# Moving ten loads of folded weights behind the normalization's last store, and one subtraction two steps forward, in a fused attention and MLP kernel

## The chip, the cores and the metric

The kernel runs on one core of a Trainium2 chip. The metric is the device time of one execution in microseconds (us); the number given for a kernel is the median of its runs. Five engines work side by side, each through its own queue in order: TensorE (PE in the profile; PEld is its weight load), VectorE (DVE), ScalarE (ACT), GpSimd (POOL) and SyncE (SP), which here issues all DMAs.

## The reference

A token row of x (2048 tokens, 640 features) is normalized twice over, and the sum of the input, a linear attention and an MLP is returned, all in float32:

```python
x = A_x
xn = _layernorm(x, axis=-1)
return x + _A_ref(xn, A_wqkv, A_w_phi, A_wo) + _B_ref(xn, B_w1, B_b1, B_w2, B_b2)
```

`_B_ref` normalizes again, multiplies by w1 (640 x 1728), applies gelu and multiplies by w2 (1728 x 640). `_A_ref` projects to q, k and v (32 heads of 20), and takes features of q and k:

```python
pq = jnp.einsum("bhsd,hdf->bhsf", q, w_phi)
phi_q = jnp.concatenate([_softmax(pq, axis=-1), _softmax(-pq, axis=-1)], axis=-1)
kv = jnp.einsum("bhsf,bhsd->bhfd", phi_k, v)
num = jnp.einsum("bhqf,bhfd->bhqd", phi_q, kv)
```

and divides num by the matching sum of features, before the last projection wo.

## The kernel before

Every float32 operand is split into a high and a low part, and a product is three matmuls (high by high, high by low, low by high; `mm3`, lines 62 to 64). Tokens are held transposed, in four blocks of 512. The program has three stages:

- **The MLP of blocks 0 and 1**, up to about 217 us. The hidden layer is cut in chunks of 128 columns, two to a group; groups 2 to 5 are done by `cycle` with fewer products (sums of weights and of tokens), group 6 by the plain `passes`. In `second`, five products of a group go to the PSUM banks 5, 6 and 7 in turn, and VectorE adds each to `acc` (line 312), which frees the bank: the fourth product waits for the first addition, the fifth for the second.
- **The projections and features of all tokens**, to about 450 us. Their first products read `wkh` and `wkl`, the two tiles of `wkv_`.
- **The MLP of blocks 2 and 3 beside the attention, and the output.**

In the first stage the order of PE, VectorE, ScalarE and GpSimd is as the code is traced; only SyncE's order is set by a scheduler from the dependencies. Side work is written as generators: PE's code calls `next(mlp.beside)` after each three matmuls, and one such step lets the side work trace a few instructions. `prep` is such a side work and runs through groups 2 to 6. It does, in this order:

- **The subtraction** (line 680): `wpt` holds w_phi of all heads (loaded at line 576); VectorE subtracts its first column from the others. Before it `prep` lets four steps go by.
- **The folds** (`folds`): PE multiplies pieces of wk and wq (`raw`, line 581) with `wpt` (line 611), ScalarE and VectorE split the results (lines 629 and 631), and SyncE stores them to DRAM (`wk_dram`, `wq_dram`, line 636).
- **The normalization of blocks 2 and 3**, ten pieces of 128 features by 512 tokens. A piece is loaded (line 673) into one of three `raw` buffers; GpSimd subtracts the mean (line 694), VectorE multiplies by the scale (702), ScalarE makes the high part in `xs` (708), VectorE the low part in place (711), and SyncE stores both to `y_dram` (line 713), the high part (`yh`) first. The load of a piece takes the buffer of the piece three before it, so it waits for that one's low store (`yl`). The pieces are called first to tenth below.

Beside the last of `prep` runs `last_weights`, in group 6. For each of five rows kc it loads the V part of the weights (line 820, `wkl<-wv`), splits it on ScalarE and VectorE (lines 502 and 505), and loads the folded high and low parts of wk from DRAM (line 823, `wkh<-wkh` and `wkl<-wkl`, 256 KB each), ten loads in all. Behind them on SyncE come the folded weights of wq (line 856).

Each DMA signals one of eight semaphores (DMAHW0 to DMAHW7), in turn, and waits until the DMA eight before it, which had the same one, has landed.

Of the kernel before, what the change touches and what calls it, by code (L numbers as in the profile page):

```python
# [25 lines left out]
F1, F2 = 16 * H, 3 * H  # L26
CB = [F1, F1 + 2 * F2 + 15 * DH, F1 + 2 * F2 + D]
# [11 lines left out]
def f(ap):  # L39
    return ap.bitcast(F32)  # L40
# [3 lines left out]
def tile_kernel(ctx: ExitStack, tc: tile.TileContext, x, xT, wkT, wqT, wv, wphi, wo, w1, b1, w2, b2,  # L44
                ident, mmask, emask, vsel, out):
    nc = tc.nc
# [33 lines left out]
    y_dram = [[tc.dram_tile([P, KC, 512], F32, name=f"y{p}{b}") for p in "hl"] for b in range(2)]  # L80
    wq_dram = [tc.dram_tile([P, KC, F1], F32, name=f"wq{p}") for p in "hl"]
    wv_dram = tc.dram_tile([P, KC, D], F32, name="wv_")
    wk_dram = [tc.dram_tile([P, KC, F1], F32, name=f"wk{p}") for p in "hl"]
# [40 lines left out]
    def stats(ts, xp, xbs, turned=False):  # L124

        t0, n = ts[0], len(ts)
        st = xp.tile([P, n, 2, 6], F32, name="st", bufs=1 if n == 8 else 2)
        for i, (t, xb) in enumerate(zip(ts, xbs)):
            for h in range(2):
                nc.vector.bn_stats(st[:, i, h, :], xb[:, h * 320:(h + 1) * 320])  # L130
            nc.vector.bn_aggr(mv[:, t, :], st[:, i, :, :])
            yield


        ts = slice(t0, t0 + n)
        q = xp.tile([P, 2, n], F32, name="q", bufs=2)
        nc.vector.tensor_scalar(q[:, 1, :], mv[:, ts, 1], 0.25 * (1 + EPS), 0.25 * EPS * EPS, op0=ALU.mult, op1=ALU.add)
        nc.vector.tensor_scalar(q[:, 0, :], mv[:, ts, 1], 0.25, 0.25 * EPS, op0=ALU.mult, op1=ALU.add)
        yield

        sr = xp.tile([P, 2, n], F32, name="sr", bufs=3)
        rr = xp.tile([P, 2, n], F32, name="rr", bufs=2)
        nc.scalar.activation(sr, q, AF.Sqrt)
        nc.vector.reciprocal(rr, sr)
        nc.vector.tensor_tensor(rr, rr, q, op=ALU.mult)
        if turned:
            nc.vector.scalar_tensor_tensor(sr, sr, -1.0, rr, op0=ALU.mult, op1=ALU.subtract)
        else:
            nc.vector.tensor_tensor(sr, sr, rr, op=ALU.add)
        nc.vector.reciprocal(ry[:, ts], sr[:, 1, :])  # L150
        yield
        ra = xp.tile([P, n], F32, name="ra", bufs=2)
        nc.vector.reciprocal(ra, sr[:, 0, :])
        nc.vector.tensor_tensor(rs_all[:, ts], sr[:, 1, :], ra, op=ALU.mult)
# [27 lines left out]
    def rows(xp, ptile):  # L182

        sc = xp.tile([P, 2, 2, 4], F32, name="sc", bufs=1)
        nc.vector.tensor_copy(sc[:, :, 0, :], mv[:, 8:16, 0].rearrange("p (b t) -> p b t", b=2))
        nc.vector.tensor_copy(sc[:, :, 1, :], ry[:, 8:16].rearrange("p (b t) -> p b t", b=2))
        for _ in range(4):
            yield
        ps = ptile()
        nc.tensor.transpose(ps[:16, :P], sc.rearrange("p b a t -> p (b a t)"), idt)  # L190
        sr = xp.tile([16, P], F32, name="sr16", bufs=1)
        nc.vector.tensor_copy(sr, ps[:16, :P])
        nc.sync.dma_start(r_dram, sr)

    def row_pair(b, mr):

        nc.sync.dma_start(mr, r_dram[8 * b - 16:8 * b - 8].rearrange("r t -> (r t)").unsqueeze(0).to_broadcast([P, 8 * P]))
        return mr.rearrange("p (a t) -> p a t", a=2)
# [126 lines left out]
    def finish(p):  # L325
        for _ in p:
            pass
# [164 lines left out]
    def at_steps(*events):  # L492

        n = 0
        for when, what in sorted(events, key=lambda e: e[0]):
            while n < when:
                n += 1
                yield
            what()

    def hi(t, src, eng=None):
        return lambda: nc.scalar.activation(t[0], src, AF.Copy)

    def lo(t, src, eng):
        return lambda: eng.tensor_tensor(t[1], src, f(t[0]), op=ALU.subtract)
# [72 lines left out]
    def raws(n, g):  # L578
        raw = fp.tile([P, D], F32, name="raw")
        if g < 5:  # L580
            nc.sync.dma_start(raw, {"k": wkT, "q": wqT}[n][g * G6:g * G6 + P, :])
        else:
            nc.sync.dma_start(raw[:2 * DH], wkT[5 * G6:])
            nc.sync.dma_start(raw[2 * DH:], wqT[D - P + 2 * DH:])
        return raw
# [64 lines left out]
    def ahead(loads, n):  # L650

        todo, ready = iter(loads), []
        for _ in loads:
            while len(ready) <= n:
                load = next(todo, None)
                if load is None:
                    break
                ready.append(load())
            yield ready.pop(0)

    def more_stats():

        def load(t):
            xb = fp.tile([P, D], F32, name="xs", bufs=3)
            nc.sync.dma_start(xb, x[t * P:(t + 1) * P, :])
            return xb

        yield from stats(range(8, 16), fp, ahead([lambda t=t: load(t) for t in range(8, 16)], 2))

    def prep():  # L670
        def load(b, c):
            xc = fp.tile([P, D], F32, name="raw")[:, :512]
            nc.sync.dma_start(xc, xT[c * P:(c + 1) * P, b * 512:(b + 1) * 512])
            return xc

        todo = [(b, c) for b in range(2, 4) for c in range(KC)]
        loads = ahead([*(lambda job=job: raws(*job) for job in jobs), *(lambda job=job: load(*job) for job in todo)], 1)
        for _ in range(4):
            yield
        nc.vector.tensor_tensor(wpt[:, :, :, 1:], wpt[:, :, :, 1:], wpt[:, :, :, 0:1].to_broadcast([P, 6, 6, DF]), op=ALU.subtract)  # L680
        more = chain(more_stats(), rows(fp, mlp.px))
        for i, _ in enumerate(folds(loads)):
            if i % 10 in (5, 7, 9):
                next(more, None)
            yield
        fs.close()
        finish(more)
        mrs = [row_pair(b, fp.tile([P, 2, 512], F32, name="t", bufs=2).rearrange("p a c -> p (a c)")) for b in range(2, 4)]
        for _ in range(6):
            yield  # L690

        def centred(b, c):
            xc = next(loads)
            nc.gpsimd.tensor_tensor(xc, xc, mrs[b - 2][:, 0], op=ALU.subtract)
            return xc

        following = centred(*todo[0])
        for _ in range(4):
            yield
        for i, (b, c) in enumerate(todo):  # L700
            xc = following
            nc.vector.tensor_tensor(xc, xc, mrs[b - 2][:, 1], op=ALU.mult)  # L702
            yield
            if i + 1 < len(todo):
                following = centred(*todo[i + 1])
            yield
            hi = fp.tile([P, D], F32R, name="xs", bufs=3)[:, :512]
            nc.scalar.activation(hi, xc, AF.Copy)
            for _ in range(2):
                yield  # L710
            nc.vector.tensor_tensor(xc.bitcast(F32R), xc, f(hi), op=ALU.subtract)  # L711
            for p, src in enumerate((f(hi), xc)):
                nc.sync.dma_start(y_dram[b - 2][p][:, c, :], src)
            for _ in range(4):
                yield

# [8 lines left out]
    def cycle(g, other, side):  # L725
# [78 lines left out]
        return mlp.second(g, 1, parts, ws)  # L804

    before, side = p11, prep()
    for g in range(2, 6):
        before = cycle(g, before, side)
# [2 lines left out]
    kvw = wkv.enter_context(tc.tile_pool(name="wkv", bufs=1, side="right", reuse_waits="tile"))  # L811
    wkv_ = [kvw.tile([P, KC, CB[2]], F32R, name=f"wk{p}") for p in "hl"]

    def last_weights():

        events = []
        for kc in range(KC):
            k, v = slice(0, F1), slice(F1 + 2 * F2, CB[2])
            raw = f(wkv_[1][:, kc, v])
            events += [(2 * kc, lambda kc=kc, raw=raw: nc.sync.dma_start(raw, wv_dram[:, kc])),  # L820
                       (2 * kc + 7, hi([wkv_[0][:, kc, v]], raw)),
                       (2 * kc + 8.5, lo([wkv_[0][:, kc, v], wkv_[1][:, kc, v]], raw, nc.vector)),
                       *((2 * kc + 10 + p, lambda kc=kc, p=p: nc.sync.dma_start(f(wkv_[p][:, kc, k]), wk_dram[p][:, kc])) for p in range(2))]
        return at_steps(*events)

    mlp.beside = both(last_weights(), side)
    ws = [ready[c][0] for c in (12, 13)]
    for b in range(2):
# [33 lines left out]
    for i in range(2):  # L862
        v = vp.tile([P, 11 * VS], F32R, name=f"v{i}")
# [121 lines left out]
    for t, i in [(t, i) for t in range(13) for i in range(4)] + [(13, 0), (13, 1), (13, 2), (14, 0), (14, 1), (13, 3), (14, 2), (15, 0), (15, 1),  # L985
                                                                  (14, 3), (15, 3), (15, 2)]:
        if (t, i) in ((4, 0), (8, 0)):
            b = t // 4 + 1
# [27 lines left out]
        if i == 0 and t in (1, 2, 3, 6, 7):  # L1016

            kc = (1, 2, 3, 6, 7).index(t)
# [536 lines left out]
```

## Time and profile before

| | us |
|---|---|
| median of 3 runs | 716.82 (716.45 to 717.29) |
| the profiled execution | 716.18 |
| its span, first to last instruction | 714.4 |
| PE busy | 701.8 (98%) |
| VectorE, GpSimd, ScalarE busy | 507.7, 434.5, 353.0 |

In the profile's rows a line is a start (us from the span's start), a duration (us), an engine, a line of the kernel, an operation and its tiles (out<-in); in brackets stands how long the engine had been idle before it, and whose work ended that. SPq is SyncE's queue: an entry is the issue of a DMA and not its transfer. Buffer numbers are left out of names: `raw` is any of its three buffers, and `bank` any PSUM bank. In the chain of waits a DMA's length goes from its issue to its landing.

### The profile page before, as it was taken

Reading aid. Unit: us, or ns where it says so; the run is one execution under the profiler, and the core shown is the slowest. Engines: PE = TensorE matmul, PEld = TensorE weight load, DVE = VectorE, ACT = ScalarE, POOL = GpSimd, SP = SyncE. Lnnn points to the kernel's source line nnn. Section 1 sums busy time; section 2 is a strip of 40 time slices with the busy share of each in tenths; the row PEclk is TensorE's granted clock in tenths of the full one; section 3 lists DMA queues with packets and bytes.
Section 4 is the critical chain, followed back from the end, with each engine's and each line's share of the span. In section 5 each row is a group of like instructions: output and inputs, shape, how many; then the busy total and the mean of one; then the engine's idle time right before and its main releaser. Section 6 shows DMA issues by size and latency. Waiting matters only on the chain.

```text
span 714.4 us, 9919 instructions
## 1 busy us (share of the span) xinstructions
PE 701.8 (98%) x3368; PEld 592.1 (83%) x3368; DVE 507.7 (71%) x842; ACT 353.0 (49%) x624; POOL 434.5 (61%) x405
## 2 busy tenths in 40 slices
PE   8999999999899999999999999999999999999998
PEld 7887888878678888888888888888888888888886
DVE  7876775597474788888978887745565646778653
ACT  7843546445433464454445547556565556551310
POOL 2576424675231897797787879656677777563400
PEclk9999999999999999999999999999999999999999
DMA  9615968456753223624600705674444753163222
GB/s 333 259 40 182 268 186 233 112 179 213 284 200 129 82 79 153 167 93 166 147 2 1 184 1 189 151 220 131 132 120 128 206 150 112 42 232 124 89 74 88
DMA packets 77895, 105.05 MB, mean 147 GB/s; under 512 B 22885, under 2 KB 46069, under 8 KB 76221
## 3 DMA queue, kind: packets, MB, share of 16 engines
q1 hardware_dynamic: 77844, 104.43, 46.3%
q8 instruction: 26, 0.43, 0.2%
q14 instruction: 25, 0.20, 0.1%
HBM read 71.43 MB, written 34.61 MB: 148 GB/s over the span
## 4 chain that ended last, share of the span: by engine, by line
PE 85%; DVE 5%; issue 3%; DMA 3%; ACT 2%; POOL 2%; POOLq 0%; ACTq 0%; SPq 0%; DVEq 0%
PE bank L62 25%; PE bank L63 25%; PE bank L64 25%; PE bank L946 3%; PE bank L611 2%; PE bank L1175 1%; PE bank L1174 1%; DMA raw<-in_xT 1%; DMA wkl<-wv__79 1%; DVE st L130 1%; PE bank L307 1%; PE bank L308 1%; DVE m L754 1%; DVE raw L711 1%; DVE raw L702 1%
## 5 line engine op out<-in xcount | busy, mean ns | idle before, releaser
L62 PE MATMUL bank<-m,w 128*128 128x512 f32 x266 | 105.5, 397 | 5.0 <-DVE acc L312 4.7
L62 PE MATMUL bank<-y,w 128*128 128x512 f32 (+1 forms) x270 | 105.1, 389 | 0.0
L63 PE MATMUL bank<-y,w 128*128 128x512 f32 (+1 forms) x270 | 104.9, 389 | 0.0
L64 PE MATMUL bank<-y,w 128*128 128x512 f32 (+1 forms) x270 | 104.8, 388 | 0.0
L64 PE MATMUL bank<-m,w 128*128 128x512 f32 x266 | 103.7, 390 | 0.0
L63 PE MATMUL bank<-m,w 128*128 128x512 f32 x262 | 102.1, 390 | 0.0
L312 DVE TENSOR_TENSOR acc<-bank,acc 128x512 f32<-128x512 f32 x120 | 80.9, 681 | 18.8 <-PE bank L64 13.8
L62 PE MATMUL bank<-wkh,y 128*128 128x512 f32 (+2 forms) x240 | 87.6, 365 | 0.0
L63 PE MATMUL bank<-wkl,y 128*128 128x512 f32 (+2 forms) x240 | 87.1, 363 | 0.0
L64 PE MATMUL bank<-wkh,y 128*128 128x512 f32 (+2 forms) x240 | 86.9, 362 | 0.0
L911 POOL TENSOR_TENSOR m<-m,mx 128x640 f32<-128x640 f32 (+2 forms) x48 | 44.6, 942 | 42.7 <-DVE mx L899 42.7
L892 ACT ACTIVATE m<-bank 128x512 f32<-128x512 f32 (+1 forms) x64 | 26.4, 439 | 85.7 <-PE bank L64 62.4
L62 PEld LDWEIGHTS bank<-m,w 128*128 128x128 f32 x266 | 50.0, 188 | 17.3 <-DVE acc L312 6.8
L1168 POOL TENSOR_TENSOR e<-e,m 128x512 fp32r<-128x512 f32 (+1 forms) x28 | 40.0, 1431 | 38.4 <-ACT m L1167 32.3
L64 PEld LDWEIGHTS bank<-y,w 128*128 128x128 f32 x270 | 51.1, 189 | 10.4
L63 PEld LDWEIGHTS bank<-y,w 128*128 128x128 f32 x270 | 51.1, 189 | 10.3
L62 PEld LDWEIGHTS bank<-y,w 128*128 128x128 f32 x270 | 51.0, 189 | 10.4
L64 PEld LDWEIGHTS bank<-m,w 128*128 128x128 f32 x266 | 49.9, 188 | 10.5
L918 DVE TENSOR_REDUCE sm<-m 128x64 f32<-128x1280 f32 x32 | 47.3, 1479 | 15.9 <-ACT m L916 15.6
L63 PEld LDWEIGHTS bank<-m,w 128*128 128x128 f32 x262 | 49.3, 188 | 9.5
L916 ACT ACTIVATE m<-m,rs_all 128x1280 f32<-128x1280 f32 x32 | 43.8, 1368 | 22.0 <-POOL m L911 21.9
L56 POOL TENSOR_TENSOR w<-r,w 128x640 fp32r<-128x640 f32 x31 | 48.5, 1583 | 7.8 <-ACT w L53 7.6
(260 smaller groups left out, 1638.2 us busy)
## 6 DMA issues: line engine op xcount, KB each, us to landing
r<-in_w SPq DMA_DIRECT2D x43, 320.0 KB
e<-e SPq DMA_DIRECT2D x40, 256.0 KB
e<-acc SPq DMA_DIRECT2D x52, 160.0 KB
acc<-in_xT SPq DMA_DIRECT2D x4, 1280.0 KB
a<-in_w SPq DMA_DIRECT2D x9, 320.0 KB
xb<-in_x SPq DMA_DIRECT2D x8, 320.0 KB
xs<-in_x SPq DMA_DIRECT2D x8, 320.0 KB
raw<-in_xT SPq DMA_DIRECT2D x10, 256.0 KB
```

The source lines that it names most:

```text
L56: eng.tensor_tensor(lo, src, f(hi), op=ALU.subtract)
L62: nc.tensor.matmul(ps, lh, rh, start=first, stop=False, **kw)
L63: nc.tensor.matmul(ps, lh, rl, start=False, stop=False, **kw)
L64: nc.tensor.matmul(ps, ll, rh, start=False, stop=last, **kw)
L312: nc.vector.tensor_tensor(acc[b][:, m, :], pw, acc[b][:, m, :], op=ALU.add)
L611: nc.tensor.matmul(ps[:, c + i * kd:c + (i + 1) * kd], raw[n, g][:, (kc + i) * P:(kc + i + 1) * P], wpt[:, g, :kd // DF, 1:], start=True, ...
L892: return nc.scalar.activation(p3[:, :, c], ps.rearrange("p (h f) -> p h f", h=H), AF.Copy).ins
L911: subs[n, t] = nc.gpsimd.tensor_tensor(ep[:, s], a, b, op=ALU.subtract)
L916: exps[n, t] = nc.scalar.activation(e, e, AF.Exp, scale=rs_all[:, t:t + 1])
L918: nc.vector.tensor_reduce(sm, e.rearrange("p s (h f) -> p (s h) f", f=DH), axis=AX, op=ALU.add)
L946: nc.tensor.matmul(kvp[g // 2][:P, (g % 2) * 240:(g % 2) * 240 + 240].rearrange("p (s f) -> p s f", s=4), v[:, g * VS:g * VS + P], ft[:, : ...
L1168: nc.gpsimd.tensor_tensor(pl, e, f(ph), op=ALU.subtract)
```

## The change

Two edits. The subtraction on `wpt` is made after two of the four steps that `prep` lets go by, instead of after all four. And the ten loads of folded wk weights are now issued behind the normalization's last store: `prep` notes each store in `stored`, and the loads are traced four steps later than before and with `issue_after`, which puts them behind the store that was noted last on SyncE's queue. No instruction is added or taken away.

```diff
+    stored = [None]
+
     def prep():
...
-        for _ in range(4):
+        for _ in range(2):
             yield
         nc.vector.tensor_tensor(wpt[:, :, :, 1:], wpt[:, :, :, 1:], wpt[:, :, :, 0:1].to_broadcast([P, 6, 6, DF]), op=ALU.subtract)
+        for _ in range(2):
+            yield
         more = chain(more_stats(), rows(fp, mlp.px))
...
             for p, src in enumerate((f(hi), xc)):
-                nc.sync.dma_start(y_dram[b - 2][p][:, c, :], src)
+                stored[0] = nc.sync.dma_start(y_dram[b - 2][p][:, c, :], src).ins
...
+    def load_k(kc, p):
+        def go():
+            with tc.issue_after(stored[0]):
+                nc.sync.dma_start(f(wkv_[p][:, kc, :F1]), wk_dram[p][:, kc])
+        return go
+
     def last_weights():
...
-            k, v = slice(0, F1), slice(F1 + 2 * F2, CB[2])
+            v = slice(F1 + 2 * F2, CB[2])
...
-                       *((2 * kc + 10 + p, lambda kc=kc, p=p: nc.sync.dma_start(f(wkv_[p][:, kc, k]), wk_dram[p][:, kc])) for p in range(2))]
+                       *((2 * kc + 14 + p, load_k(kc, p)) for p in range(2))]
```

On VectorE, at the beginning of the folds (`wpt` is the tile of the subtraction, `acc` the MLP's sum):

```order
 L310 SCALAR_TENSOR_TENSOR acc_103<-bank_768,b2t,acc_103 128x512
 L310 SCALAR_TENSOR_TENSOR acc_103<-bank_780,b2t,acc_103 128x512
+L682 TENSOR_TENSOR wpt<-wpt 128x36x19
 L312 TENSOR_TENSOR acc_103<-bank_800,acc_103 128x512
-L680 TENSOR_TENSOR wpt<-wpt 128x36x19
 L631 TENSOR_TENSOR t<-bank_822,t 128x384
```

The subtraction has moved in front of one addition to `acc`. Before both stand the same two additions of line 310.

On SyncE, at the end of the normalization, before the change, with the semaphores that each waits for. The first row is the seventh low store, the row of L673 the tenth load, and the two rows of L713 around it are the eighth high and low stores:

```order
L713 DMA yl_76<-raw 128x512 [waits DMAHW1_49,DVE_49]
L820 DMA wkl<-wv__79 128x640
L823 DMA wkh<-wkh 128x512 [waits DMAHW3_49,Pool_49]
L823 DMA wkl<-wkl 128x512 [waits DMAHW4_49]
L823 DMA wkh<-wkh 128x512 [waits DMAHW5_49]
L823 DMA wkl<-wkl 128x512 [waits DMAHW6_49]
L713 DMA yh_75<-xs 128x512 [waits DMAHW7_49,Activation_49]
L823 DMA wkh<-wkh 128x512 [waits DMAHW0_49]
L823 DMA wkl<-wkl 128x512 [waits DMAHW1_49]
L673 DMA raw<-in_xT 128x512 [waits DMAHW2_49]
L713 DMA yl_76<-raw 128x512 [waits DMAHW3_49,DVE_49]
```

Four more of L823 and the last four stores follow. After the change, from the same store:

```order
L717 DMA yl_76<-raw 128x512 [waits DMAHW1_49,DVE_49]
L830 DMA wkl<-wv__79 128x640
L717 DMA yh_75<-xs 128x512 [waits DMAHW3_49,Activation_49]
L675 DMA raw<-in_xT 128x512 [waits DMAHW4_49,DMAHW1_49]
L717 DMA yl_76<-raw 128x512 [waits DMAHW5_49,DVE_49]
L717 DMA yh_75<-xs 128x512 [waits DMAHW6_49,Activation_49]
L717 DMA yl_76<-raw 128x512 [waits DMAHW7_49,DVE_49]
L717 DMA yh_75<-xs 128x512 [waits DMAHW0_49,Activation_49]
L717 DMA yl_76<-raw 128x512 [waits DVE_49]
L821 DMA wkh<-wkh 128x512 [waits DMAHW2_49,Pool_49]
L821 DMA wkl<-wkl 128x512 [waits DMAHW3_49]
```

All ten loads of folded weights (L823, now L821) stand behind the tenth low store, eight more after these two. The tenth load of `raw` stands behind one store instead of six of these loads and a store, and waits itself for the seventh low store (DMAHW1), which the load in front of it waited for before. The lines of code after the change are shifted by up to ten.

## Prediction

> **What bounds the kernel now.** I read the page first, then who TensorE (PE) waited for, then the timelines around those waits.
>
> ```profile
> PE 701.8 (98%) x3368; PEld 592.1 (83%) x3368; DVE 507.7 (71%) x842; ACT 353.0 (49%) x624; POOL 434.5 (61%) x405
> ```
>
> PE is busy 98% of a span of 714.4 us, so only its stops, and stretches where it runs slowly, can be won. The list of PE's waits names two kinds in the region of the change (in us, times, longest):
>
> ```profile
> PE bank L62 <- DVE acc L312: 4.7, 3, 3.3
> PE bank L611 <- issue: 1.7, 1, 1.7
> ```
>
> The first place is where the folds begin. PE's and VectorE's timelines (start, duration, operation, idle before it):
>
> ```profile
> 65.59 0.39 PE L64 MATMUL bank<-th,w 128*128 128x512 f32 x1
> 67.65 2.01 PE L611 MATMUL bank<-wpt,raw 128*128 128x114 f32 x16 [1.68 <-issue]
> 69.43 0.48 PE L62 MATMUL bank<-th,w 128*128 128x512 f32 x1
> ...
> 76.10 0.39 PE L64 MATMUL bank<-th,w 128*128 128x512 f32 x1
> 76.33 1.93 PE L611 MATMUL bank<-wpt,raw 128*128 128x114 f32 x16
> 78.03 0.48 PE L62 MATMUL bank<-th,w 128*128 128x512 f32 x1
> ```
>
> ```profile
> 62.38 1.40 DVE L310 SCALAR_TENSOR_TENSOR acc<-bank,b2t,acc 128x512 f32<-128x512 f32 x2
> 65.34 0.69 DVE L312 TENSOR_TENSOR acc<-bank,acc 128x512 f32<-128x512 f32 x1 [1.56 <-PE bank L64]
> 65.94 1.61 DVE L680 TENSOR_TENSOR wpt<-wpt 128x684 f32<-128x684 f32 x1
> ```
>
> The first fold product starts at 67.65, and the subtraction L680 ends at 65.94 + 1.61 = 67.55. The profile names no releaser ("issue"), but the 0.10 us between them makes it L680. Ahead of L680 VectorE stood idle for 1.56 us, waiting for PE so that it could do L312. The second fold group shows what is normal: 0.23 us after the matmul before it, and 1.70 us long instead of 1.78.
>
> The second place is the end of the normalization. PE:
>
> ```profile
> 189.78 0.39 PE L62 MATMUL bank<-m,w 128*128 128x512 f32 x1
> ...
> 190.91 0.39 PE L64 MATMUL bank<-m,w 128*128 128x512 f32 x1
> 192.34 0.50 PE L62 MATMUL bank<-m,w 128*128 128x512 f32 x1 [1.04 <-DVE acc L312]
> ...
> 197.33 0.50 PE L62 MATMUL bank<-m,w 128*128 128x512 f32 x1 [3.33 <-DVE acc L312]
> ```
>
> VectorE, which PE waits for there:
>
> ```profile
> 189.80 0.69 DVE L702 TENSOR_TENSOR raw<-raw,t 128x512 f32<-128x512 f32 x1 [6.57 <-POOL raw L694]
> ...
> 191.01 0.68 DVE L288 TENSOR_TENSOR m<-bank,m 64x512 f32<-64x512 f32 x1
> 191.61 0.67 DVE L312 TENSOR_TENSOR acc<-bank,acc 128x512 f32<-128x512 f32 x1
> 194.91 1.77 DVE L711 TENSOR_TENSOR raw<-raw,xs 128x512 fp32r<-128x512 f32 x1 [2.62 <-ACT xs L708]
> 196.60 0.68 DVE L312 TENSOR_TENSOR acc<-bank,acc 128x512 f32<-128x512 f32 x1
> ```
>
> In PE's order each L312 frees a bank; in VectorE's order both stand behind the tenth and last piece of the normalization (L702, then L711), which stands behind GpSimd's L694 of that piece. GpSimd, and the chain of waits (start, length):
>
> ```profile
> 176.58 1.30 POOL L694 TENSOR_TENSOR raw<-raw,t 128x512 f32<-128x512 f32 x1 [3.61 <-DVE acc L312]
> 188.46 1.30 POOL L694 TENSOR_TENSOR raw<-raw,t 128x512 f32<-128x512 f32 x1 [10.59 <-DMA raw<-in_xT]
> ```
>
> ```profile
> 0.74 3.08 DMA xb<-in_x
> ...
> 175.42 7.58 DMA wkl<-wv__79
> 183.02 5.28 DMA raw<-in_xT
> ```
>
> So a late DMA holds PE: the tenth load of raw is issued at 183.02 and lands 5.28 us later, at 188.30. The first load of the program, with nothing before it, took 3.08. The stops also cost speed afterwards; the table by stretches (length, busy times, granted clock, DMA share, GB/s):
>
> ```profile
> 64.00:70.00 6.00, 4.33 (x28) 3.61 (x27) 2.76 (x4) 2.12 (x5) 4.72 (x5) 1.00 0.89 322
> ...
> 198.00:203.00 5.00, 5.00 (x17) 3.93 (x16) 5.00 (x7) 1.80 (x3) 3.12 (x5) 0.66 0.74 281
> ```
>
> After the stop of 1.68 the clock stays at 1.00. After those of 1.04 and 3.33 it is 0.66 over 5 us: 5 x 0.34 = 1.7 us of PE's work lost.
>
> **The change part by part.** All times are on the axis of before until the sum.
>
> *The subtraction.* It moves in front of one L312. VectorE ends the two L310 at 62.38 + 1.40 = 63.78 and is then free; what it subtracts from was sent for 25 us earlier:
>
> ```profile
> L576 SPq DMA_DIRECT2D wpt<-in_wphi x1: 328/328/328, 38.6 to 38.6; - x1
> ```
>
> The subtraction runs from 63.78 to 65.39 at its 1.61, inside the 1.56 of idle time. The L312 behind it starts at 65.39 instead of 65.34, which nobody feels: no wait of PE is listed on it. PE may begin L611 at 65.39, before it comes there at 65.59 + 0.23 = 65.82. Next in line are the raw weights:
>
> ```profile
> 61.05 2.24 SPq L581 DMA_DIRECT2D raw<-in_wkT x3
> ```
>
> The three are issued by 63.29; with 3.08 each the second is there by about 65.7 and the third by 66.4, while the second is read by the sixth of eight products, 5 x 0.22 after 65.82, and the third by a later group. Gain: 67.65 - 65.82 = 1.83, and 1.78 - 1.70 = 0.08 in the group: 1.9 us. Bounds: 0 (something else holds L611) to 1.9. No loss: L312 is 0.05 later at most. What follows has to come earlier too; its vector work hangs on PE's products, step by step, so I carry the 1.9 to the end.
>
> *The ten loads of folded weights.* SyncE's queue around the tenth load (the order of both is in the section on the change):
>
> ```profile
> 171.57 0.34 SPq L673 DMA_DIRECT2D raw<-in_xT  x1
> ...
> 174.47 0.91 SPq L713 DMA_DIRECT2D yl<-raw  x1
> 175.42 0.65 SPq L820 DMA_DIRECT2D wkl<-wv__79  x1
> 176.50 0.32 SPq L823 DMA_DIRECT2D wkh<-wkh  x1
> ...
> 182.24 0.32 SPq L823 DMA_DIRECT2D wkl<-wkl  x1
> 183.02 0.33 SPq L673 DMA_DIRECT2D raw<-in_xT  x1
> ...
> 186.36 0.32 SPq L823 DMA_DIRECT2D wkl<-wkl  x1
> ...
> 196.71 0.32 SPq L713 DMA_DIRECT2D yl<-raw  x1
> ```
>
> Six of the ten stand in front of the tenth raw load and leave. Its issue then waits for its buffer, that is for the seventh low store (issued 174.47); that store had landed by 182.24, since the L823 issued there waits for the same semaphore. New issue: 182.3, won 0.7. Ahead of it in the DMA queues remain the last load of wv (landed 183.00 by the chain) and one 256 KB store. From 183.00 to 188.30 eight transfers of 256 KB passed (six loads, a store, the raw load), 0.66 each, so that store is out of the way at 183.7; the floor of 3.08 rules, and the load lands at 182.3 + 3.08 = 185.4, won 2.9. Bounds: the ninth load, issued 171.57 with three wv loads right behind it, was in use at 176.58, so it took up to 5.0; at 5.0 the tenth lands at 187.3 and wins 1.0. At best it lands as soon as the queue lets it through, one transfer behind the store, at 184.3, and wins 4.0. I take 3.08: what stands behind the tenth now are stores, one at a time.
>
> From there all shifts by 2.9: L694 185.6, L702 186.9, L288 188.1 (its input from ScalarE comes at 187.9, below), first L312 188.7, L711 192.0, second L312 193.7.
>
> ```profile
> 187.26 0.60 ACT L287 ACTIVATE m<-bank 64x512 f32<-64x512 f32 x1 [0.85 <-PE bank L285]
> ```
>
> PE wants its fourth group at 190.91 + 0.23 = 191.14: the stop of 1.04 is gone. Six matmuls of 0.227 (189.78 to 190.91 holds five steps) bring it to the fifth at 192.50, and L312 frees that at 194.4: a stop of 1.9 stays. The fifth group comes at 197.33 - 2.9 = 194.4; the rest of the stop is what is late next, L711 behind ScalarE's L708.
>
> *The cover of the moved loads.* They now stand behind the tenth low store, which moves to 196.71 - 2.9 = 193.8. Ten at 0.66 after a floor of 3.08 land by about 203.5. PE reads them first here:
>
> ```profile
> 217.47 0.39 PE L62 MATMUL bank<-wkh,y 128*128 128x512 f32 x1
> ```
>
> 217.47 less 4.6 is 212.9: 9 us of cover, so I cost this at nothing. The two loads of wq behind them have three products more.
>
> *The clock.* The remaining stop of 1.9 lies near the 1.68 that left the clock at 1.00, and far from 1.04 + 3.33. I take no loss: 1.7 us won; the bounds are 0 and 1.7.
> The Trainium skill (TensorE: Matmul & The Clock Gate, "What's actually happening") says that the array falls to half rate after an idle window of about 3.4 us, and that the windows run freely. The trace agrees in part: the clock fell here though the longest stop was 3.33. By that rule a stop of 1.9 keeps the full clock and the sum is -6.5; were the row's threshold as low as 1.9, it would be -4.8.
>
> *The sum.* 1.9 + 2.9 + 1.7 = 6.5 us. The profiled execution took 716.18 (span 714.4 and 1.8 around it) and comes to 709.7. The median of the three runs shown is 716.82, 0.64 above it, so I forecast 716.82 - 6.5 = **710.3**.
>
> **The rivals.**
> - *The clock still falls.* The stop of 1.9 would do what 1.04 + 3.33 did. For it: nothing between 1.68 and 3.33 is in the trace. Then 716.82 - 4.8 = 712.0. Chance 0.25.
> - *The tenth load is in flight for 5.0 again.* For it: the ninth. Against it: the ninth had five other loads close behind it, and the tenth has none. Then 2.9 becomes 1.0, the stop is 192.50 to 196.3, and the clock falls: 716.82 - 1.9 - 1.0 = 713.9. Chance 0.12.
> - *The 1.9 us are given back before 170.* L611 may have waited for its raw weights, or a vector chain that was just in time may not follow; in its third, shortest wait on L312 (4.7 - 3.33 - 1.04 = 0.3) PE was already held by VectorE. Against it: that chain starts from PE's own products. Then 716.82 - 4.6 = 712.2. Chance 0.08.
> - *No change.* The load is not earlier, because the seventh store lands later than its semaphore order suggests, and the 1.9 are lost too: 716.8. Chance 0.03.
> - *Slower: the folded weights come too late for the projection.* If the ten go one after another, each with a flight of its own, 10 x 3.08 after 193.8 ends at 224.6, while the last pair is read 4 x 3 x 0.227 = 2.7 after 212.9, at 215.6: a stop of 9.0, and 1.7 of clock behind it: 716.82 - 6.5 + 10.7 = 721.0. It decides from (215.6 - 193.8) / 10 = 2.2 us a load on. Against it: 0.66 each in the queue of before, and each waits only for the DMA eight in front of it. Chance 0.04.
>
> **How the numbers follow.** The forecast has 0.48. A measurement of this kernel tells about 0.2%, 1.4 us, from no change; all cases but the last two lie beyond it on the fast side: faster 0.93, same 0.03, slower 0.04. The range reaches from 709.2 (the load as early as the queue allows, 4.0 instead of 2.9) over the two cases at 712 to 713.2, which leaves out half of the late load's case and the last two.
>
> **What would show it.** In the profile of the changed kernel PE's wait on "issue" at L611 is gone, and L611 starts 0.23 after the matmul before it; VectorE's subtraction lies at 63.8. The tenth raw load is issued 0.7 earlier against its surroundings and POOL's idle time before the last L694 falls from 10.59 to about 7.7. PE's waits on L312 sum to about 2.2 instead of 4.7, with one of 1.9 where two were, and the clock there stays at 1.00. I am wrong if the clock falls there again, if POOL's wait stays over 9, or if PE waits for the folded weights at the projection.

## The result, and the profile after

The changed kernel took 710.66 us (median of 4 runs, 710.05 to 712.57) against 716.63 for the kernel before beside it (4 runs, 716.18 to 717.29): a ratio of 0.992, interval 0.990 to 0.9941. The forecast was 710.3 in a range of 709.2 to 713.2. The profiled execution took 710.79, with a span of 708.9 instead of 714.4. PE's waits (us in total, times, longest):

```profile
PE bank L62 <- DVE acc L312: 2.6, 2, 2.2
...
PE bank L1185 <- POOL e L1178: 0.5, 2, 0.3
```

The wait on "issue" at L611 is gone, and the waits on L312 fell from 4.7 to 2.6 in total. The first place, on PE and on VectorE (start, duration, operation):

```profile
65.59 0.39 PE L64 MATMUL bank<-th,w 128*128 128x512 f32 x1
65.82 1.93 PE L611 MATMUL bank<-wpt,raw 128*128 128x114 f32 x16
67.52 0.48 PE L62 MATMUL bank<-th,w 128*128 128x512 f32 x1
```

```profile
63.69 0.86 DVE L682 TENSOR_TENSOR wpt<-wpt 128x684 f32<-128x684 f32 x1
```

L611 starts 0.23 after the matmul before it, at 65.82 instead of 67.65, and the group behind it at 67.52 instead of 69.43: 1.91 us. The second place: SyncE's issues, the chain of waits, GpSimd's last L698 (L694 before) with its idle time, VectorE, PE.

```profile
172.64 0.89 SPq L717 DMA_DIRECT2D yl<-raw  x1
...
180.37 0.33 SPq L675 DMA_DIRECT2D raw<-in_xT  x1
...
192.39 0.32 SPq L717 DMA_DIRECT2D yl<-raw  x1
192.81 0.38 SPq L821 DMA_DIRECT2D wkh<-wkh  x1
```

```profile
172.64 7.72 DMA yl<-raw
...
180.37 3.60 DMA raw<-in_xT
```

```profile
184.13 1.29 POOL L698 TENSOR_TENSOR raw<-raw,t 128x512 f32<-128x512 f32 x1 [8.07 <-DMA raw<-in_xT]
```

```profile
185.46 0.69 DVE L706 TENSOR_TENSOR raw<-raw,t 128x512 f32<-128x512 f32 x1 [4.05 <-POOL raw L698]
...
187.27 0.67 DVE L312 TENSOR_TENSOR acc<-bank,acc 128x512 f32<-128x512 f32 x1
190.58 1.78 DVE L715 TENSOR_TENSOR raw<-raw,xs 128x512 fp32r<-128x512 f32 x1 [2.64 <-ACT xs L712]
192.29 0.68 DVE L312 TENSOR_TENSOR acc<-bank,acc 128x512 f32<-128x512 f32 x1
```

```profile
190.39 0.39 PE L64 MATMUL bank<-m,w 128*128 128x512 f32 x1
193.02 0.50 PE L62 MATMUL bank<-m,w 128*128 128x512 f32 x1 [2.25 <-DVE acc L312]
```

The tenth load is issued at 180.37 instead of 183.02, 2.65 earlier: 1.89 from the first part and 0.76 of its own. It is in flight for 3.60 instead of 5.28 and lands at 183.97 instead of 188.30, which is 4.33 - 1.89 = 2.44 won by the moved loads. The stop of 1.04 is gone, the one of 3.33 is 2.25, and the fifth group starts at 193.02 instead of 197.33. The ten folded loads are issued behind the last store, and the first product of theirs waits for nothing:

```profile
211.52 0.39 PE L62 MATMUL bank<-wkh,y 128*128 128x512 f32 x1
```

That is 217.47 - 211.52 = 5.95 earlier than before; 4.31 of it was there at the fifth group, so 1.64 came in between. The table by stretches says from where: two stretches of 3.41 us each, one with most of the stop in it and the one behind it, before (first fence) and after (length, the busy time of PE, PEld, VectorE, ScalarE and GpSimd, then the granted clock ahead of the DMA share and GB/s).

```profile
195.44:198.85 3.41, 1.52 (x7) 1.27 (x8) 3.41 (x3) 3.41 (x6) 2.88 (x3) 1.00 0.42 156
198.85:202.26 3.41, 3.41 (x10) 2.63 (x9) 3.41 (x6) 0.95 (x2) 2.66 (x4) 0.50 0.79 294
```

```profile
191.32:194.73 3.41, 1.71 (x7) 1.42 (x8) 3.41 (x3) 3.41 (x5) 2.68 (x3) 1.00 0.66 196
194.73:198.14 3.41, 3.41 (x16) 2.81 (x15) 3.41 (x7) 0.74 (x2) 2.68 (x4) 1.00 0.97 334
```

Before, PE ran at exactly 0.50 for one such stretch, which costs 3.41 / 2 = 1.7; after, it did not. Later 0.5 us are lost again. ScalarE's first copy of the attention's input waits longer for its load than before (first fence before, second after), 4.58 instead of 3.42, and PE waits 0.5 in all for GpSimd behind it (L1185 above) instead of 0.2:

```profile
471.10 0.63 ACT L1167 ACTIVATE m<-e 80x512 fp32r<-80x512 f32 x1 [3.42 <-DMA e<-e]
```

```profile
466.31 0.63 ACT L1177 ACTIVATE m<-e 80x512 fp32r<-80x512 f32 x1 [4.58 <-DMA e<-e]
```

The copy thus starts only 4.79 earlier. The sum by the traces is 1.9 + 2.4 + 1.7 - 0.5 = 5.5, the difference of the spans.

### The profile page after: what moved, and what is told of

Its sections match the earlier page's. It is cut to its first block, busy times and chain, and to the rows that moved or that the text cites. A ratio compares the mean times of both kernels' runs of the same rounds, so it can differ in the third digit from the quotient of the medians.

```text
span 708.9 us, 9921 instructions
## 1 busy us (share of the span) xinstructions
PE 700.8 (99%) x3368; PEld 591.9 (83%) x3368; DVE 511.4 (72%) x842; ACT 353.1 (50%) x624; POOL 433.1 (61%) x405
## 4 chain that ended last, share of the span: by engine, by line
PE 82%; DVE 5%; DMA 4%; issue 4%; POOL 2%; ACT 2%; SPq 0%; POOLq 0%; ACTq 0%; DVEq 0%
PE bank L62 25%; PE bank L63 24%; PE bank L64 24%; PE bank L956 3%; PE bank L1185 1%; PE bank L611 1%; PE bank L1184 1%; DMA yl<-raw 1%; DMA raw<-in_xT 1%; DVE st L130 1%; DMA e<-e 1%; PE bank L308 1%; PE bank L307 1%; DVE raw L715 1%; DVE m L758 1%
## 5 line engine op out<-in xcount | busy, mean ns | idle before, releaser
L312 DVE TENSOR_TENSOR acc<-bank,acc 128x512 f32<-128x512 f32 x120 | 80.9, 681 | 17.3 <-PE bank L64 12.4
```

The lines of the kernel that those rows point to most:

```text
L312: nc.vector.tensor_tensor(acc[b][:, m, :], pw, acc[b][:, m, :], op=ALU.add)
```

## The experiments

My theory was the forecast's: the two parts add up, the queue in front of the tenth load made it late, its landing set PE's stops, and the clock follows the stops. The rivals are named with each run. Each time stands beside that of the kernel before from the same chip (medians of 716.0, 716.0 and 716.63).

### The subtraction alone

```diff
-        for _ in range(4):
+        for _ in range(2):
             yield
         nc.vector.tensor_tensor(wpt..., op=ALU.subtract)
+        for _ in range(2):
+            yield
```

> Only the subtraction on phi's weights is moved two steps forward; the folded loads stand where the kernel before has them. Theory: the stall of 1.83 us at the first fold product goes and nothing later takes it back, so the time falls by the 1.9 us that the changed kernel's trace shows at that place, from about 716.6 to 714.7; TensorE still stops twice in front of the last accumulator additions (about 1.0 and 3.3 us) and the clock still falls behind them. Rival: the 1.9 us are waited away again in front of the tenth raw load, whose store and loads come no earlier: 716.6.

Measured: 714.8 (714.12 to 717.09, 12 runs) against 716.0, ratio 0.9986, interval 0.9975 to 0.9998. PE:

```profile
65.79 1.93 PE L611 MATMUL bank<-wpt,raw 128*128 128x114 f32 x16
...
190.31 0.50 PE L62 MATMUL bank<-m,w 128*128 128x512 f32 x1 [0.98 <-DVE acc L312]
...
195.31 0.51 PE L62 MATMUL bank<-m,w 128*128 128x512 f32 x1 [3.33 <-DVE acc L312]
```

The fifth group comes 197.33 - 195.31 = 2.02 earlier and both later stops are as before: the part is real and is carried through, and the spans of the two profiles differ by 714.4 - 712.3 = 2.1. The medians show only 1.2 of it, and the clock explains a part of the gap. One step of 3.41 us at half speed costs 1.7 of 714 us and so brings a run's mean clock to 0.997 or 0.998; two would bring it to about 0.995 (an estimate from that). The runs with 0.997 or 0.998 alone have medians of 714.5 here (9 of 12) and 716.1 before (14 of 19), 1.6 apart. The lower clock of two such steps stands in 3 of the 12 runs here and in 1 of the 19, and a clock of 0.999 or 1.000 in none here and in 4 of the 19, which took 714.36 to 714.64. The last 0.3 are not explained.

### The loads alone

The diff of the change without its part in the subtraction.

> Only the folded loads are moved; the subtraction stands where the kernel before has it. Theory: the tenth raw load lands 2.4 us earlier against the work around it, TensorE's two stops become one of about 2.25 us, and the clock stays at 1.00, which is worth another 1.7 us; with the 0.5 us that the changed kernel loses again at the start of the attention this gives 716.6 - 2.4 - 1.7 + 0.5 = 713.0, and with the run of the subtraction alone the two parts add up to the whole change. Rival (the clock has nothing to do with the loads and is won by the subtraction, or falls all the same): 716.6 - 2.4 = 714.2 or later, with the granted clock at 0.50 somewhere between 190 and 205 us.

Measured: 713.65 (711.72 to 714.14, 8 runs) against 716.0, ratio 0.9963, interval 0.9949 to 0.9977. PE:

```profile
67.63 2.01 PE L611 MATMUL bank<-wpt,raw 128*128 128x114 f32 x16 [1.68 <-issue]
...
194.60 0.50 PE L62 MATMUL bank<-m,w 128*128 128x512 f32 x1 [1.92 <-DVE acc L312]
```

The fifth group comes 2.73 earlier with one stop of 1.92, the old stop at L611 stays, and the clock stayed in this profile. But the eight times form two groups: 711.72, 711.92 and 712.23 with a clock of 0.999 or 1.000, four from 713.85 to 714.14 with 0.997 or 0.998, and 713.45 with 1.000, which I can't place. The clock is not settled by the kernel alone. Among the runs that kept 0.999 or 1.000 the medians are 714.4 for the kernel before (6 of the 37 beside all experiments), 712.1 here (4) and 710.4 for the changed kernel (8 of its 11): 2.3 for the loads and 4.0 for the whole change. With the 1.6 of the subtraction alone the two parts add up.

### The folded loads right behind the tenth load

```diff
+            loaded[0] = nc.sync.dma_start(xc, ...).ins      # each raw load is noted
...
-            with tc.issue_after(stored[0]):
+            with tc.issue_after(loaded[0]):      # the tenth raw load
```

> As the changed kernel, but the ten folded loads are queued right behind the tenth raw load instead of behind the last store. Theory: only what stands in front of the tenth raw load in the queue delays it; its flight stays at about 3.6 us, TensorE's stop at about 2.25 us and the time at that of the changed kernel, 710.7. Rival: loads queued behind it take their share of the DMA engines while it flies, as the ninth raw load with three weight loads right behind it flies about 5 us; then the tenth lands 1.3 us later, the stop grows to about 3.6 us, the clock falls behind it, and the time is 712 to 713.8.

Measured: 711.38 (709.88 to 712.72, 6 runs), ratio 0.994, interval 0.9922 to 0.9957. SyncE and GpSimd:

```profile
180.61 0.33 SPq L675 DMA_DIRECT2D raw<-in_xT  x1
```

```profile
184.49 1.30 POOL L698 TENSOR_TENSOR raw<-raw,t 128x512 f32<-128x512 f32 x1 [8.20 <-DMA raw<-in_xT]
```

From issue to GpSimd's start it is 3.88 where the changed kernel has 3.76, and the stop is 2.52: the landing is the same, and what counts is what stands in front. Three of the six runs have a clock of 0.997 or 0.998. But here a store of the eighth piece slipped in between, and the first folded load follows the tenth raw load by more than a microsecond; the next experiment but one shows what closer ones do.

### Four of the ten in front again

```diff
-                       *((2 * kc + 14 + p, load_k(kc, p)) for p in range(2))]
+                       *((2 * kc + (10 if kc < 2 else 14) + p, load_k(kc, p)) for p in range(2))]
```

> The changed kernel, but four of the ten folded loads stand in front of the tenth raw load again (before the change there were six). Theory: the bytes in front of the tenth load in the queue set its landing, 0.66 us for each load that has not drained; two fewer than before makes 1.3 us of the 2.4, so it lands 1.1 us later than in the changed kernel, the stop grows from 2.25 to about 3.3 us, and the time is 711.6 where the clock stays and 713.3 where it falls. Rival: SP waits there for a store anyway and four loads drain meanwhile; then the landing, the stop and the time are the changed kernel's.

Measured: 713.44 (712.44 to 714.42, 6 runs) against 716.0, ratio 0.9963, interval 0.9949 to 0.9978.

```profile
185.37 1.30 POOL L698 TENSOR_TENSOR raw<-raw,t 128x512 f32<-128x512 f32 x1 [9.36 <-DMA raw<-in_xT]
```

```profile
194.25 0.50 PE L62 MATMUL bank<-m,w 128*128 128x512 f32 x1 [3.35 <-DVE acc L312]
```

```profile
191.56:194.97 3.41, 0.72 (x3) 0.62 (x4) 3.15 (x3) 3.41 (x6) 3.27 (x3) 1.00 0.37 138
194.97:198.38 3.41, 3.41 (x10) 2.63 (x9) 3.41 (x5) 1.74 (x3) 2.60 (x3) 0.50 0.98 288
```

GpSimd starts 1.24 later than in the changed kernel (1.1 expected), the stop is 3.35 (3.3 expected), and the clock fell for one stretch. Four loads in front cost 1.2 and six cost 2.4, so the queue in front of the load sets its landing.

### V's weights behind the tenth load as well

```diff
...
-    events += [(2 * kc, lambda kc=kc, raw=raw: nc.sync.dma_start(raw, wv_dram[:, kc])),
+    events += [(2 * kc, load_v(kc, raw)),      # the same under issue_after(loaded[0])
```

> The changed kernel with the five loads of V's weights put behind the tenth raw load as well. Theory: the seventh piece's low store lands about 4 us earlier, so the tenth load is issued at about 176 us instead of 180.4 and lands at about 180; but the addition that TensorE waits for stands behind the tenth piece's low part, and that behind ScalarE's copy and TensorE's own work, so the stop shrinks only from 2.25 to about 1.4 us and the time is about 709.9, with fewer falls of the clock. Rival: the flight of the tenth load is still what sets the stop: it goes altogether, and the time is 708.4.

Measured: 709.85 (709.57 to 710.25, 5 runs), ratio 0.9913, interval 0.990 to 0.9925. SyncE, GpSimd, VectorE, PE:

```profile
174.43 0.33 SPq L675 DMA_DIRECT2D raw<-in_xT  x1
```

```profile
179.37 1.56 POOL L698 TENSOR_TENSOR raw<-raw,t 128x512 f32<-128x512 f32 x1 [4.95 <-DMA raw<-in_xT]
```

```profile
181.48 0.68 DVE L706 TENSOR_TENSOR raw<-raw,t 128x512 f32<-128x512 f32 x1
187.09 0.69 DVE L312 TENSOR_TENSOR acc<-bank,acc 128x512 f32<-128x512 f32 x1
190.28 1.80 DVE L715 TENSOR_TENSOR raw<-raw,xs 128x512 fp32r<-128x512 f32 x1 [2.49 <-ACT xs L712]
192.01 0.68 DVE L312 TENSOR_TENSOR acc<-bank,acc 128x512 f32<-128x512 f32 x1
```

```profile
192.74 0.50 PE L62 MATMUL bank<-m,w 128*128 128x512 f32 x1 [1.60 <-DVE acc L312]
```

The tenth piece is there 4.8 us earlier than in the changed kernel, and the stop shrinks by 0.65. The flight of the load was no longer what held PE: the rival falls. A by-product: with V's loads right behind it the tenth load needs 4.94 from issue to GpSimd's start, not 3.76. The first of those loads is issued 0.4 us behind it. So loads close behind seem to slow a load, on this one comparison; in the run with the folded loads right behind the tenth they were 1.2 us off.

### VectorE's order turned

```diff
             nc.scalar.activation(hi, xc, AF.Copy)
-            for _ in range(2):
+            for _ in range(2 if i + 1 < len(todo) else 6):
                 yield
             nc.vector.tensor_tensor(xc.bitcast(F32R), xc, f(hi), op=ALU.subtract)
```

> The changed kernel with one more edit: VectorE's low part of the tenth piece (and with it that piece's low store and the folded loads behind it) is put behind the next two accumulator additions. Theory: the stop of 2.25 us that is left in the changed kernel is no longer the flight of the tenth load, but the addition that stands on VectorE behind the low part, which waits for ScalarE's copy of the tenth piece; with the order turned the addition runs at once, the stop goes, no run shows a lower clock, and the time is 710.7 - 2.2 = 708.5. Rival: TensorE waits just as long for a later addition or for the split of V's weights that is now pushed back, and the time stays within 0.5 us of 710.7.

Measured: 707.89 (707.45 to 709.13, 5 runs), ratio 0.9889, interval 0.9872 to 0.9906: the best version here. VectorE:

```profile
187.04 0.67 DVE L312 TENSOR_TENSOR acc<-bank,acc 128x512 f32<-128x512 f32 x1
188.12 0.69 DVE L312 TENSOR_TENSOR acc<-bank,acc 128x512 f32<-128x512 f32 x1 [0.41 <-PE bank L64]
...
194.57 0.68 DVE L715 TENSOR_TENSOR raw<-raw,xs 128x512 fp32r<-128x512 f32 x1
```

The second L312 now waits for PE instead of PE for it; PE has no stop of 0.3 us or more between 160 and 230 us. The gain on the median of the changed kernel is 710.66 - 707.89 = 2.8; on its eight runs that kept their clock (710.4) it is 2.5, near the stop of 2.25. No run here lost its clock.

### That order, with the loads left where they were

The kernel before with the subtraction moved and the edit of the last experiment; the folded loads stay in front of the tenth raw load.

> The kernel before with the subtraction moved and the tenth piece's low part put behind the next two accumulator additions, while the folded loads stand where they were, in front of the tenth raw load. Theory: the late tenth load costs only the stop of 1.0 us in front of the fourth group; the stop of 3.33 us behind it came from the order on VectorE and goes, and the clock stays: 714.6 - 3.3 - 1.7 = 709.6. Rival: the loads had to move: both stops of the run with the subtraction alone stay or become one of 3 us or more, the clock falls, and the time is 712 or more.

Measured: 709.75 (709.61 to 710.53, 5 runs) against 716.0, ratio 0.9913, interval 0.990 to 0.9926. GpSimd, VectorE and PE:

```profile
186.48 1.29 POOL L696 TENSOR_TENSOR raw<-raw,t 128x512 f32<-128x512 f32 x1 [10.51 <-DMA raw<-in_xT]
```

```profile
189.62 1.27 DVE L312 TENSOR_TENSOR acc<-bank,acc 128x512 f32<-128x512 f32 x2
```

```profile
190.34 0.50 PE L62 MATMUL bank<-m,w 128*128 128x512 f32 x1 [0.97 <-DVE acc L312]
```

The tenth load is as late as ever, and only the stop of 0.97 is left of the two. The stop of 3.33 needed the low part in its place on VectorE: with the addition in front it is gone, though the load is late. Against the subtraction alone this order is worth 714.8 - 709.75 = 5.0, the stop and the 1.7 of the clock. With the loads moved too, the stop of 0.97 goes as well, with another of 0.65 at 203 us, and the time falls by a further 709.75 - 707.89 = 1.9.

### The folded loads later still

```diff
...      # the loads of the changed kernel are taken out of last_weights
     for p in range(2):
-        nc.sync.dma_start(f(wq_[p]), wq_dram[p])
+        last_wq = nc.sync.dma_start(f(wq_[p]), wq_dram[p]).ins
+    for kc in range(KC):
+        for p in range(2):
+            with tc.issue_after(last_wq):
+                nc.sync.dma_start(f(wkv_[p][:, kc, :F1]), wk_dram[p][:, kc])
```

> The changed kernel, but the ten folded loads go still later on SyncE, behind the two loads of the query weights. Theory: they have about 8 us of cover where the change put them; the two query loads of 1.25 MB each take 6.6 us at 0.66 per 256 KB, so the folded loads land between about 207 and 213 us, each still in front of its first product (first one at 211.5, one more pair each 0.7 us): the time stays within 0.7 us of the changed kernel's, about 711. Rival: each load takes 2.2 us or more of its own where it stands, as the forecast's slower case had it; then TensorE waits for folded weights in front of the projection and the time is 715 or more.

Measured: 710.06 (709.75 to 711.39, 4 runs) against 716.63, ratio 0.9916, interval 0.990 to 0.9933. SyncE's last folded load, and PE's first product with them:

```profile
203.35 0.32 SPq L863 DMA_DIRECT2D wkl<-wkl  x1
```

```profile
210.96 0.39 PE L62 MATMUL bank<-wkh,y 128*128 128x512 f32 x1
```

By the trace's records of completion the first nine loads end one after another, 0.68 us apart, from 202.7 to 208.1, and the last at 210.1; PE waits for none. The slower case needed 2.2 a load; it falls.

### The changed kernel again

> The changed kernel itself, once more, with more runs. Theory: whether the clock falls behind a stop depends on where the stop lies in steps of 3.41 us that begin at another moment in each execution (in the traces so far the clock changed only whole steps after it had come up), so a stop of 2.25 us lets it fall in a part of the runs: the times come in two groups 1.7 us apart, about 710.4 and 712.2, a third to a half of them in the upper one. Rival: the single run at 712.57 was a disturbance, and all runs lie within 0.5 us of 710.5.

Measured: 711.56, 710.89, 710.16, 711.76 and 711.62 against 716.0, ratio 0.9931, interval 0.9918 to 0.9945. The last two have a clock of 0.997. The first kept 1.000; in its profile PE waits 0.8 at the attention's start and 0.2 at L611 for the raw weights. So there are runs with and without the fall, though closer together than 1.7.

> The changed kernel, for one more profile of the stop of about 2.25 us and of the clock behind it. Theory: the clock falls if the stop covers more than about 1.9 us of one of the steps of 3.41 us that count from the moment when the clock came up in this execution (in the profiles so far it fell with 1.89, 2.07 and 2.70 us of idle time in one step and stayed with 1.63, 1.70, 1.76 and 1.93). Rival: the length of the stop alone decides, and the clock stays here as in both profiles of this kernel so far.

> As the look before: the clock falls if and only if the stop covers more than about 1.9 us of one step of 3.41 us; the rival says that it stays whatever the step.

Measured: 710.12 and 710.27. The stops were 2.08 and 2.00, of which 1.59 and 1.37 lay in one step, and the clock stayed. Both theories allow that; these two profiles decide nothing.

## Why the prediction was right, and where it was off

**The subtraction.** Forecast 1.9, measured 1.91, and carried on to 185 us as assumed. Its own duration was 0.86, not 1.61; the idle time hid either. The raw weights, which the prediction named as next in line, are indeed close: in one of the four profiles of the changed kernel PE waits 0.2 for them.

**The tenth load.** Its issue was forecast 0.7 earlier and came 0.76 earlier. The flight was forecast at the floor of 3.08 and measured 3.60, so 2.44 were won instead of 2.9: the term was 0.5 too large, and POOL's idle time was 8.07, not 7.7. The rival with 5.0 did not come; what it stood on is real, though: with loads close behind it, the flight was about 4.8 in the run with V's weights moved.

**The remaining stop.** Forecast 1.9, measured 2.25 in this profile and 2.00 to 2.29 in the three others of the same kernel. "L711 behind ScalarE's L708" was what the prediction named as late next. It was more than that: turning the order without moving the loads took all of the 3.33 away, while the earlier load alone took 1.08. The prediction read the chain rightly, back to the load, but did not ask how long the second L312 would be held with the load on time.

**The clock.** Taking no loss was right in the profile and in 8 of the 11 runs of the changed kernel; in 3 the granted clock is 0.997, and the rival at 712.0 with its chance of 0.25 is what those runs did (711.62, 711.76 and 712.57). Before, too, the loss was no fixed 1.7: by the mean clock, 6 of 37 runs lost nothing (median 714.4), 23 one step (716.0) and 8 probably two (717.0). The step "the remaining stop of 1.9 lies near the 1.68 that left the clock at 1.00" is the weak one: it treats the length of a stop as deciding. In all 13 profiles the first stretch at full clock lasted a whole number of steps of 3.413 us (194.56 = 57 steps before, 187.73 = 55 in the run with four loads), from a start that lies between 4.3 and 7.2 us. The clock fell behind a step in which PE stood idle for 3.41 - 1.52 = 1.89 (before), 2.07 (subtraction alone) and 2.69 (four loads); it stayed behind 3.41 - 1.71 = 1.70 (after) and at most behind 1.93:

```profile
189.37:192.78 3.41, 1.48 (x7) 0.90 (x5) 1.84 (x2) 3.41 (x7) 3.27 (x3) 1.00 1.03 396
192.78:196.19 3.41, 2.82 (x12) 2.36 (x13) 3.41 (x4) 3.05 (x5) 1.64 (x3) 1.00 0.90 274
```

That is the run with the folded loads right behind the tenth. The end of the program, where PE runs out of work, agrees: with the order alone turned the clock fell behind a step with 3.41 - 1.44 = 1.97 idle,

```profile
703.22:706.63 3.41, 1.44 (x13) 1.23 (x11) 0.53 (x2) 0.00 (x0) 0.00 (x0) 1.00 0.27 92
706.63:710.04 3.41, 0.00 (x0) 0.00 (x0) 0.00 (x0) 0.00 (x0) 0.00 (x0) 0.50 0.01 2
```

and in one profile of the changed kernel it stayed there behind 1.81. So the border lies at about 1.9 us of idle time in one step, and not sharply, since the clock fell behind 1.89 and stayed behind 1.93 of these modelled times. A stop of length s that begins anywhere in a step puts 1.9 into one step with an estimated chance of (3.41 - s + 2 x (s - 1.9)) / 3.41, which is 0.86 for 3.33, 0.55 for 2.25, 0.45 for 1.92 and 0 below 1.9. Runs with a mean clock of 0.998 or less:

| kernel | stops in its profile, us | runs |
|---|---|---|
| before | 1.04 and 3.33 | 31 of 37 |
| subtraction alone | 0.98 and 3.33 | 12 of 12 |
| four loads in front | 3.35 | 5 of 6 |
| behind the tenth load | 2.52 | 3 of 6 |
| changed kernel | 2.25, 2.29, 2.08, 2.00 | 3 of 11 |
| loads alone | 1.92, and 1.68 at L611 | 4 of 8 |
| folded loads later still | 1.85 | 1 of 4 |
| V's weights; order alone; order turned | 1.60; 0.97; none | 0 of 15 |

The order of the rows fits roughly, though the numbers are small and a stop varies by some tenths from run to run; the border rests on three falls in mid-kernel and on the ends, and no profile caught a fall behind a stop of 2.0 to 2.5. The Trainium skill (TensorE: Matmul & The Clock Gate, "What's actually happening") gives a free-running window of 3413 ns and two states, half and full; the traces agree with both. It has the clock fall after at least one idle window, and there they differ: 1.89 of 3.41 were enough.

**The sum.** 6.5 forecast on the medians, 716.63 - 710.66 = 5.97 measured; 6.5 against 5.5 on the profiles. The load's flight makes 0.5 of that, and the 0.5 at the attention's start makes the rest. ScalarE's wait there is 4.10 to 4.92 in the six profiles in which SyncE has the order of the changed kernel, the folded loads behind the last store (the four of the changed kernel, the loads alone, the order turned), and 2.93 to 3.69 in the seven others. So it seems to go with the place of these loads, though they are done some 260 us before it; what links the two was not tried and stays open.

The nearness of 710.66 to 710.3 is in part luck. The later runs have medians of 716.0 for the kernel before (37) and 710.79 for the changed one (11), 5.2 apart: the base of 716.82 was 0.8 too high and the gain 1.3 too large, and the two partly offset each other. Without the clock, the forecast's gain was 1.9 + 2.9 = 4.8, and the runs that kept their clock show 4.0.

**Cover.** Right, with room left: the loads could move behind the query weights without a wait.

## What to carry to other kernels

When an engine waits for an instruction that stands behind a late one in another engine's order, ask first whether it has to stand there: turning the order on VectorE was worth more than hurrying the load, and the two together were worth most. A load that another engine waits for belongs in front of loads that are needed 20 us later, and each 256 KB still ahead of it in the queue cost about 0.66 us. A stop of two to three microseconds costs its clock in some executions and not in others, so price it with a chance, and look at several runs before calling the clock safe.

## What the runs showed of the hardware

GpSimd around the subtraction, in the changed kernel:

```profile
61.26 1.51 POOL L505 TENSOR_TENSOR w<-sraw,w 128x128 fp32r<-128x128 f32 x1
65.28 1.55 POOL L505 TENSOR_TENSOR w<-r,w 128x640 fp32r<-128x640 f32 x1 [2.51 <-ACT w L502]
```

The same subtraction took 0.86 us at 63.69, in GpSimd's pause, and 1.61 at 65.94 before, beside GpSimd's operations with two inputs, the first of which stands at the same time there; the low part of the tenth piece took 1.78 beside GpSimd's work and 0.68 without it, in the run with VectorE's order turned. The Trainium skill (GPSIMD Engine Reference, "1. Specifications") says that GpSimd's SBUF interfaces are shared with VectorE and contend with VectorE's instructions of two SBUF inputs; the numbers agree, and moving a VectorE step into GpSimd's pause took about half of its duration away.
